# A contiguous 256 KiB head for each tensor in a streaming x + alpha * fx

## The chip, the cores and the metric

The kernel runs on one core of one Trainium2 chip. The metric is the device time of one execution in microseconds, as the median of several runs. A separate profiled execution gives the profile; its span runs from the core's first to its last instruction and is a little shorter than the time, which also holds what lies around it.

## The reference

```python
B, S, D = 512, 32, 640
# x, fx: bfloat16 of shape (B, S, D); alpha: bfloat16 of shape (1,)
def reference(x, fx, alpha):
    return x + alpha * fx
```

Each of x, fx and the output holds 10,485,760 elements, 20.97 MB. Two are read and one is written: 62.92 MB in all.

## The kernel before

**Layout.** Each tensor is seen as 128 rows of 81,920 contiguous elements, one row for each partition of the on-chip memory. A row is counted in units of K = 512 elements (1 KiB): it is ROW = 160 units long, 160 KiB, and that is also the distance in DRAM from one partition's row to the next. All numbers in the plan are such units.

**One buffer.** There is a single tile `t` (L77) of 160 + 47.5 = 207.5 units per partition. x 0 to 160 lies at places 0 to 160, the sum is written over x, and the output is stored from there. fx has no place of its own: each piece is loaded to a place that x does not need yet, or no longer needs, and `lies` remembers where it went. So fx 0 to 65 lies at 95 to 160, where x 95 to 160 is to come; fx 65 to 112.5 lies in the spare room from 160 to 207.5; and later pieces overwrite earlier ones there.

**An order written out by hand.** The string PLAN (L27 to L55) gives the program order, one step to a line, and each engine runs its own steps in this order:

- `f a b p` loads fx from a to b to place p (L99 to L101), `x a b` loads x (L96, L97), `s a b` stores (L119, L120). All of these, and the load of alpha, are issued by SP (SyncE) and go through one DMA queue. A load over a place that is still read, and a store of a sum that is not there yet, wait on SP, and everything behind them on SP waits too.
- `a` loads alpha (L103 to L111): its one element goes to 8 partitions, a 1 x 1 matrix multiplication with a row of ones on TensorE spreads it over 128 partitions, and VectorE copies it out of PSUM (L111).
- `m a b` multiplies fx by alpha in place on VectorE (L113, L114), and `c a b` adds it to x (L116, L117).
- `s 0 64 | m 112.5 134.5` also makes that store wait for the named multiplication (L129, L130).

The plan has three stretches. First the loads that need no room to be made: fx 0 to 8, alpha, fx 8 to 65, x 0 to 64, x 64 to 95 and fx 65 to 112.5. Then VectorE multiplies and adds piece by piece; x 95 to 112.5 and x 112.5 to 160 are issued when fx 0 to 65 has been added, and the last two pieces of fx when fx 65 to 95 and 95 to 112.5 have been. Last the stores: 0 to 64 is issued while the last loads still run, then 64 to 128, then 128 to 160. A nop on SP (L132) waits for all but the last store.

`of` (L87, L88) cuts units a to b out of a tensor in DRAM, `at` (L84, L85) cuts them out of `t`, and `place` (L90 to L94) finds where a piece of fx lies. A transfer over 128 partitions becomes 128 pieces, one for each partition, spread over 16 DMA engines, so each engine moves eight.

Of the kernel before, what the change touches and what calls it, by code (L numbers as in the profile page):

```python
# [1 line left out]

# [4 lines left out]

ALU = mybir.AluOpType
F32 = mybir.dt.float32

P = 128
K = 512
ROW = 160
SPARE = 47.5

LANES = 8

PLAN = """  # L27
f 0 8 95
a
f 8 65 103  # L30
x 0 64
x 64 95
f 65 112.5 160
m 0 8
m 8 65
c 0 8
c 8 64
c 64 65
x 95 112.5
x 112.5 160  # L40
m 65 95
c 65 95
f 112.5 142.5 160
m 95 112.5
c 95 112.5
f 142.5 160 190
m 112.5 134.5
s 0 64 | m 112.5 134.5
m 134.5 142.5
c 112.5 142.5  # L50
m 142.5 160
c 142.5 160
s 64 128
s 128 160
"""  # L55


@with_exitstack
def kernel(
    ctx: ExitStack,  # L60
    tc: tile.TileContext,
    x: bass.AP,
    fx: bass.AP,
    alpha: bass.AP,
    out: bass.AP,
):
    nc = tc.nc
    xv, fv, ov = (
        t.flatten_outer_dims().rearrange("(p n) d -> p (n d)", p=P) for t in (x, fx, out)
    )  # L70
    assert xv.shape[1] == ROW * K

    consts = ctx.enter_context(tc.tile_pool(name="consts", bufs=1))
    psum = ctx.enter_context(tc.tile_pool(name="psum", bufs=1, space=bass.MemoryType.PSUM))
    flat = ctx.enter_context(tc.tile_pool(name="flat", bufs=1))
    ctx.enter_context(tc.manual_schedule())
    t = flat.tile([P, int((ROW + SPARE) * K)], x.dtype, name="t")  # L77
    info = mybir.DependencyInfo(mybir.DependencyClass.Sync, mybir.DependencyReason.DATA)

    lanes = {}  # L80
    lies = []
    done = []

    def at(a, b):  # L84
        return t[:, int(a * K) : int(b * K)]  # L85

    def of(v, a, b):  # L87
        return v[:, int(a * K) : int(b * K)]  # L88

    def place(a, b):  # L90
        for c, d, p in reversed(lies):
            if c <= a and b <= d:
                return at(p + a - c, p + b - c)
        raise ValueError(f"fx {a} to {b} lies nowhere in one piece")  # L94

    def load_x(a, b):  # L96
        done.append(nc.sync.dma_start(out=at(a, b), in_=of(xv, a, b)))  # L97

    def load_f(a, b, p):  # L99
        lies.append((a, b, p))  # L100
        done.append(nc.sync.dma_start(out=at(p, p + b - a), in_=of(fv, a, b)))  # L101

    def load_alpha():  # L103
        a_n = consts.tile([LANES, 1], alpha.dtype, name="a_n")
        done.append(nc.sync.dma_start(out=a_n[:], in_=alpha[None, :].to_broadcast([LANES, 1])))  # L105
        ones = consts.tile([1, P], alpha.dtype, name="ones")
        nc.vector.memset(ones[:], 1.0)  # L107
        a_ps = psum.tile([P, 1], F32, name="a_ps")
        done.append(nc.tensor.matmul(a_ps[:], ones[:], a_n[0:1, :], start=True, stop=True))  # L109
        lanes["a"] = consts.tile([P, 1], F32, name="a_f")  # L110
        nc.vector.tensor_copy(out=lanes["a"][:], in_=a_ps[:])  # L111

    def multiply(a, b):  # L113
        done.append(nc.vector.tensor_scalar_mul(place(a, b), place(a, b), lanes["a"][:]))  # L114

    def add(a, b):  # L116
        done.append(nc.vector.tensor_add(at(a, b), at(a, b), place(a, b)))  # L117

    def store(a, b):  # L119
        done.append(nc.sync.dma_start(out=of(ov, a, b), in_=at(a, b)))  # L120

    does = {"x": load_x, "f": load_f, "a": load_alpha, "m": multiply, "c": add, "s": store}
    begun = {}
    for step in filter(None, PLAN.split("\n")):
        step, *later = step.split(" | ")
        what, *numbers = step.split()
        does[what](*map(float, numbers))
        begun[step] = done[-1]
        for other in later:  # L129
            tc.add_manual_dep(done[-1].ins, begun[other].ins.name, info, reason="begins late")  # L130

    rest = nc.sync.nop(nofuse=True)  # L132
    for i in done[:-1]:
        tc.add_manual_dep(rest.ins, i.ins.name, info, reason="all but the last store")


# [1 line left out]
_INS = ['x', 'fx', 'alpha']  # L138
_OUTS = [((512, 32, 640), 'bfloat16')]


# [23 lines left out]
```

## Time and profile before

| | |
|---|---|
| median of 3 runs (lowest to highest) | 151.05 us (151.03 to 151.10) |
| profiled execution | 151.06 us, of it a span of 149.3 us |
| VectorE busy | 66.5 us, 16 instructions |
| TensorE, ScalarE, GpSimd busy | 0.2 us or less each |
| DMA: HBM read and written | 41.94 MB and 20.97 MB, 421 GB/s over the span |
| fx 0 to 8, from issue to landing | 5.0 us, 1024 KB |
| fx 8 to 65, from issue to landing | 21.3 us, 7296 KB |

The DMA queue is one queue in order, so the time from issue to landing of a transfer holds the time of those ahead of it. The profile counts packets (one contiguous piece that one DMA engine moves) and says what share of time the 16 engines spent on them. Where a stretch of time is cut out, a packet is counted where it starts, so short stretches with long packets can show more or less than the true rate. Idle time of VectorE is put down to the load for which it waited.

### The profile page before, as it was taken

The page shows a single profiled execution, that of the slowest core. Times are in us where ns is not written, and L with a number is a line of the kernel's source. Part 1 is how long each engine was busy: PE and PEld are TensorE (multiplying, and loading weights), DVE is VectorE, ACT ScalarE, POOL GpSimd, SP SyncE. Part 2 cuts the span into 40 slices and gives each one's busy share as a digit, 9 for nine tenths or more (in the row PEclk, how much of TensorE's full clock was granted, in tenths as well). Part 3 has the DMA queues.
Part 4 walks back from the last instruction along what each step waited for, and adds up shares of the span by engine and source line. Part 5 has one row for each costly group of instructions (what it writes and reads, how often), then busy time and mean ns, then how long its engine had stood idle before and what let it go on. Part 6 is the DMA issues. An engine that isn't in the chain of part 4 may idle for free.

```text
span 149.3 us, 85 instructions
## 1 busy us (share of the span) xinstructions
PE 0.2 (0%) x1; PEld 0.1 (0%) x1; DVE 66.5 (45%) x16; POOL 0.2 (0%) x4
## 2 busy tenths in 40 slices
PE   0000000000000000000000000000000000000000
PEld 0000000000000000000000000000000000000000
DVE  0300008920069999029999900599997000000000
POOL 0000000000000000000000000000000000000000
DMA  5969998969699999999999799899896969697994
GB/s 149 617 266 500 500 461 351 562 281 562 281 408 442 447 417 443 456 388 565 430 417 417 340 461 461 379 516 457 386 562 281 562 281 562 281 562 334 430 439 202
DMA packets 1745, 62.92 MB, mean 421 GB/s; under 512 B 209, under 2 KB 209, under 8 KB 209
## 3 DMA queue, kind: packets, MB, share of 16 engines
q1 hardware_dynamic: 1744, 62.92, 98.1%
q14 instruction: 1, 0.00, 0.0%
HBM read 41.94 MB, written 20.97 MB: 421 GB/s over the span
## 4 chain that ended last, share of the span: by engine, by line
DMA 38%; DVE 31%; another core or an unknown queue 4%; issue 2%; SPq 1%; DVEq 0%
DMA t<-in_x_dram 27%; DVE t L117 26%; DMA t<-in_fx_dram 11%; DVE t L114 5%; SPq L101 0%; SPq L105 0%; DVEq L117 0%
## 5 line engine op out<-in xcount | busy, mean ns | idle before, releaser
L117 DVE TENSOR_TENSOR t<-t 128x15360 bf16<-128x15360 bf16 (+4 forms) x7 | 43.6, 6251 | 11.7 <-DMA t<-in_x_dram 11.6
L114 DVE TENSOR_SCALAR t<-t,a_f 128x4096 bf16<-128x4096 bf16 (+4 forms) x7 | 22.8, 3265 | 30.7 <-DMA t<-in_fx_dram 30.7
L111 DVE COPY a_f<-a_ps 128x1 f32<-128x1 f32 x1 | 0.2, 158 | 5.0 <-PE a_ps L109 5.0
L107 DVE MEMSET ones<- 1x128 bf16 x1 | 0.2, 165 | 0.8 <-PEq L149 0.8
L109 PE MATMUL a_ps<-a_n,ones 1*128 1x1 bf16 x1 | 0.2, 158 | 5.8 <-DMA a_n<-in_alpha_dram 5.8
L149 POOL MEMSET const-bfloat16-1.0<- 128x1 bf16 x1 | 0.1, 101 | 0.0
L149 POOL MEMSET const-uint8-127<- 128x1 uint8 x1 | 0.1, 101 | 0.0
L109 PEld LDWEIGHTS <-ones 1*128 1x128 bf16 x1 | 0.1, 99 | 1.0 <-DVE ones L107 1.0
L149 POOL MEMSET const-float32-0.0<- 128x1 f32 x1 | 0.1, 98 | 0.2 <-issue 0.2
L149 POOL MEMSET const-float32-1.0<- 128x1 f32 x1 | 0.1, 98 | 0.0
## 6 DMA issues: line engine op xcount, KB each, us to landing
t<-in_fx_dram SPq DMA_DIRECT2D x1, 7296.0 KB, 21.3
t<-in_fx_dram SPq DMA_DIRECT2D x1, 6080.0 KB, 63.0
t<-in_x_dram SPq DMA_DIRECT2D x1, 6080.0 KB, 25.7
out_dram<-t SPq DMA_DIRECT2D x1, 4096.0 KB, 33.7
t<-in_x_dram SPq DMA_DIRECT2D x1, 3968.0 KB, 49.2
t<-in_fx_dram SPq DMA_DIRECT2D x1, 3840.0 KB, 16.4
t<-in_x_dram SPq DMA_DIRECT2D x1, 2240.0 KB, 11.7
t<-in_fx_dram SPq DMA_DIRECT2D x1, 2240.0 KB
```

The source lines that it names most:

```text
L107: nc.vector.memset(ones[:], 1.0)
L109: done.append(nc.tensor.matmul(a_ps[:], ones[:], a_n[0:1, :], start=True, stop=True))
L111: nc.vector.tensor_copy(out=lanes["a"][:], in_=a_ps[:])
L114: done.append(nc.vector.tensor_scalar_mul(place(a, b), place(a, b), lanes["a"][:]))
L117: done.append(nc.vector.tensor_add(at(a, b), at(a, b), place(a, b)))
L149: nc = _bacc.Bacc("TRN2", target_bir_lowering=False, num_devices=1)
```

## The change

The units 0 to 2 of all 128 partitions, 2 KiB each, no longer come from the heads of 128 rows that lie 160 KiB apart. They come from the first 256 KiB of each tensor, which lie in one piece; the rest of the tensor is cut into 128 rows of 158 units, which lie 158 KiB apart. As the operation is elementwise and all three tensors are cut in the same way, the output is the same.

The first load is then fx 0 to 2 in place of 0 to 8. The second is fx 2 to 65 (it was third, as 8 to 65), and alpha comes third. x 2 to 66 is loaded ahead of x 0 to 2, and the store 2 to 66 goes ahead of the store 0 to 2, since a transfer cannot cross from the head to the rest. The multiplications are cut at 2 in place of 8; of the additions, 0 to 8, 8 to 64 and 64 to 65 become 2 to 65 and 0 to 2. Beside alpha's there were nine loads and three stores; there are now ten and four.

```diff
+HEAD = 2
...
 PLAN = """
-f 0 8 95
+f 0 2 95
+f 2 65 97
 a
-f 8 65 103
-x 0 64
-x 64 95
+x 2 66
+x 0 2
+x 66 95
 f 65 112.5 160
-m 0 8
-m 8 65
-c 0 8
-c 8 64
-c 64 65
+m 0 2
+m 2 65
+c 2 65
+c 0 2
 x 95 112.5
 x 112.5 160
 m 65 95
...
 c 95 112.5
 f 142.5 160 190
 m 112.5 134.5
-s 0 64 | m 112.5 134.5
+s 2 66 | m 112.5 134.5
 m 134.5 142.5
 c 112.5 142.5
 m 142.5 160
 c 142.5 160
-s 64 128
-s 128 160
+s 0 2
+s 66 130
+s 130 160
 """
...
-    xv, fv, ov = (
-        t.flatten_outer_dims().rearrange("(p n) d -> p (n d)", p=P) for t in (x, fx, out)
-    )
-    assert xv.shape[1] == ROW * K
+    xv, fv, ov = (t.flatten_outer_dims().rearrange("n d -> (n d)") for t in (x, fx, out))
+    assert xv.shape[0] == P * ROW * K
...
     def of(v, a, b):
-        return v[:, int(a * K) : int(b * K)]
+        assert b <= HEAD or a >= HEAD
+        at_head = b <= HEAD
+        part = v[: int(P * HEAD * K)] if at_head else v[int(P * HEAD * K) :]
+        shift = 0 if at_head else HEAD
+        return part.rearrange("(p n) -> p n", p=P)[:, int((a - shift) * K) : int((b - shift) * K)]
```

## The prediction

> **What bounds the kernel now.** I read the page first, the busy shares by slice, the one DMA queue and the chain, then the order of time, then stretches of half a microsecond at the start.
>
> ```profile
> span 149.3 us, 85 instructions
> ...
> DMA  5969998969699999999999799899896969697994
> ...
> q1 hardware_dynamic: 1744, 62.92, 98.1%
> ...
> DMA 38%; DVE 31%; another core or an unknown queue 4%; issue 2%; SPq 1%; DVEq 0%
> ```
>
> The reader is to see one queue that is full for 98.1% of the span. The chain gives 31% to VectorE, yet this does not make VectorE the bound: the chain steps through an addition because it releases a later load's issue, while the queue still has other loads to move. The lines by time show how far ahead the issues are.
>
> ```profile
> 0.73 0.38 SPq L101 DMA_DIRECT2D t<-in_fx_dram  x1
> ...
> 1.16 0.35 SPq L105 DMA_DIRECT2D a_n<-in_alpha_dram  x1
> 1.57 0.35 SPq L101 DMA_DIRECT2D t<-in_fx_dram  x1
> 1.96 1.04 SPq L97 DMA_DIRECT2D t<-in_x_dram  x2
> 3.05 0.53 SPq L101 DMA_DIRECT2D t<-in_fx_dram  x1
> ...
> 22.93 7.82 DVE L114 TENSOR_SCALAR t<-t,a_f 128x29184 bf16<-128x29184 bf16 x1 [15.49 <-DMA t<-in_fx_dram]
> 42.34 17.63 DVE L117 TENSOR_TENSOR t<-t 128x4096 bf16<-128x4096 bf16 x3 [11.60 <-DMA t<-in_x_dram]
> 59.66 0.80 SPq L97 DMA_DIRECT2D t<-in_x_dram  x2
> 66.07 4.22 DVE L114 TENSOR_SCALAR t<-t,a_f 128x15360 bf16<-128x15360 bf16 x1 [6.10 <-DMA t<-in_fx_dram]
> ```
>
> The loads issued at 59.66 stand behind fx 65 to 112.5, which lands at 66.07; so that issue has 6.4 us in hand, less the 1.0 us from an issue to its first packet (0.73 to 1.74 for the first load in the packet records). The only stretch in which the queue has work and does not run full is the first:
>
> ```profile
> 1.00:1.50 0.50, 0.00 (x0) 0.10 (x1) 0.00 (x0) 0.00 (x0) 1.00 0.00 0
> 1.50:2.00 0.50, 0.00 (x0) 0.00 (x0) 0.00 (x0) 0.00 (x0) 1.00 1.59 262
> 2.00:2.50 0.50, 0.00 (x0) 0.00 (x0) 0.00 (x0) 0.00 (x0) 1.00 0.42 82
> 2.50:3.00 0.50, 0.00 (x0) 0.00 (x0) 0.00 (x0) 0.00 (x0) 1.00 0.78 246
> 3.00:3.50 0.50, 0.00 (x0) 0.00 (x0) 0.00 (x0) 0.00 (x0) 1.00 0.85 328
> 3.50:4.00 0.50, 0.00 (x0) 0.00 (x0) 0.00 (x0) 0.00 (x0) 1.00 1.02 426
> ```
>
> The last column is GB/s: 197 on the mean from 1.5 to 3.0, 426 by 3.5. (A packet counts where it starts.) In the packet records each engine moves eight 8 KiB packets of the first load. The later ones all take about 309 ns, but the first of each engine takes 793 ns on the mean (342 to 1253), a loss of 0.48 us; all eight together lose 0.75 us on the mean, and 1.07 us on the engine that ends last (884 and 802 ns for its first two). From then on nothing is made up: engines leave the first load 0.54 us apart and end the kernel 0.6 us apart.
>
> This lets the span be rebuilt. The 64 KiB and 8 KiB packets (2418 and 309 ns) give 36.8 ns per KiB and engine, or 435 GB/s: 62.92 MB is 144.6 us. Twelve transfers of 8 packets per engine, each packet with about 5 ns more that do not depend on its size, and a semaphore write of some 10 ns per transfer, are 0.6. With 1.74 to the first packet, 1.07 of slow start, 0.36 from the last packet to its landing and 0.75 of ending this makes 149.1, against 149.3. Outside the span lie 151.06 - 149.3 = 1.76 us; the profiled execution's 151.06 stands 0.01 above the median of 151.05.
>
> **The change part by part.** *Bytes.* The same 62.92 MB move: 0.
>
> *Transfers.* Twelve large ones become fourteen (one more load of x, one more store), with three of 2 KiB packets: fx, x and out 0 to 2. Per engine that adds 16 packets and 2 semaphore writes. No 2 KiB packet is in the trace. From below, the 64 KiB rate makes it 75 ns; from above, a 4-byte packet takes 9 ns, so 75 + 9 = 84. I take 5 ns of fixed cost, as between 8 and 64 KiB: 16 x 5 + 2 x 6 = **+0.09 us** (0 to +0.17). It lies in a full queue, so it is on the path.
>
> *The start.* The first load is 256 KiB in one piece instead of 128 rows 160 KiB apart. This is the term that decides, and no row shows it. Upper end of the gain: the slowest engine's 1.07 goes, less up to 0.17 because engines start up to 0.23 us apart: 0.9. Lower end: no gain; below nothing, if the next load's first rows pay a first packet's 0.48 on top. I take neither. Two engines had first packets of 342 and 399 ns, nearly the settled time, and lost 686 and 383 ns in their second: the loss is not one fixed delay of waking up, it goes with opening rows that lie apart. The small load opens far fewer; its successor opens one row per engine. So I leave one first packet's mean loss, 0.48, and the gain is 1.07 - 0.48 = **-0.59 us**.
>
> The Trainium skill (DMA: Bandwidth & Descriptors, Latency and other measured facts) reports that 128 rows at pitches of large powers of two fall to 207 GB/s and less, and that a few KiB of padding restore the rate. Here 160 KiB runs at 435 after the start, so the trace does not bear it out beyond 3.5 us; if it were the cause of the 197, the new pitch of 158 KiB would clear all of the loss and the time would be 150.25 instead.
>
> *The second load must be there.* It moves from third issue to second: 1.16 instead of 1.57 us, first packets from 1.16 + 1.0 = 2.2. The head needs 8 x 84 ns = 0.67 us from 1.74 to 1.97, so until 2.4 to 2.6 without any slow packet. There is no gap: 0. Left behind alpha it would come at 2.6.
>
> *Alpha third.* Its packets now queue behind 8 of 63 KiB (2.32 us each), so it lands at about 22 us instead of 5.7. Behind it stand the matrix multiplication, the copy (L109, L111) and all VectorE work. The multiplications then begin at 22.9 + 0.4 for matmul and copy (5.72 to 6.15 now), with 1024 elements in 0.48 us (4096 in 1.28, 29184 in 7.82, so 0.26 ns each) and 32256 in 8.62: done by 32.5. What they feed waits until x lands at 42.3. Cover of some 10 us: 0. Without it, 0.4 + 0.48 + 8.62 - 7.82 = 1.7 us.
>
> *The additions.*
>
> ```profile
> L117 DVE TENSOR_TENSOR t<-t 128x28672 bf16<-128x28672 bf16 x1 | 15.1, 15083 | 0.0
> ...
> L117 DVE TENSOR_TENSOR t<-t 128x4096 bf16<-128x4096 bf16 x1 | 2.3, 2293 | 11.6 <-DMA t<-in_x_dram 11.6
> L117 DVE TENSOR_TENSOR t<-t 128x512 bf16<-128x512 bf16 x1 | 0.4, 416 | 0.0
> ```
>
> At 0.52 ns per element, 2 to 65 takes 16.95 and 0 to 2 takes 0.68, together 17.63, what the three took. Both loads of x that wait for their space (95 to 112.5 on both additions) issue near 60.0 instead of 59.66 and 60.04: 0.3 of 5 us in hand: 0. Behind them on SP stands only the issue at 78.5, which waits for later work anyway.
>
> *Issues.* SP issues seven loads in a row instead of six, about 0.5 us more, by some 4.1 us; the third large one is needed at 22: 0. The store 0 to 2 waits for nothing new behind store 2 to 66 at 98.1, and 66 to 130 issues at 107.5 while the queue still stores 2 to 66 until 119: 0. Later work keeps its forms and its distance to the landings.
>
> Sum: 149.3 + 0.09 - 0.59 = 148.8; with 1.76 outside, 150.56, less 0.01 for the median: **150.55 us**.
>
> **The rivals.** *The slow start is a matter of time, not of rows* (engines or memory ramp up for about 1.5 us whatever is read). For it: every engine is settled by 3.8 us, however its loss was spread. Against it: the 342 ns packet. Then only the 0.09 remains: 151.14.
>
> *The start is paid twice, the case on the other side.* The head goes through its slow packets and then the second load opens 128 fresh rows with little queued ahead. If each engine loses a mean first packet's 0.48 again, the time is 151.05 + 0.09 + 0.48 = 151.6. It decides as soon as that second loss exceeds what the head saves, less 0.09. Against it: x 0 to 64, also 128 fresh rows, shows packets of 2418 to 2472 ns, no loss; but it stood behind 17 us of packets.
>
> *Every added transfer exposes its latency.* Two more, each with 1.0 us from issue to first packet and 0.36 to landing, would be +2.7: 153.8. Against it: fx 8 to 65 landed at 22.9, 17.2 us after its forerunner, 435 GB/s with nothing between. The Trainium skill's DMA page (Anatomy of one DMA) has about 2 us fixed per DMA, so by that rule 4 us more; it speaks against small transfers, and the queue of this trace does not agree.
>
> *The change does not do what it says*: a piece of 256 KiB is cut in four packets of 64 KiB on four engines. These would move 2.42 us instead of 0.67 for each of three transfers: +5.3, 156.4. The packet count would tell.
>
> **How the numbers follow.** Forecast 0.65, of which 0.05 falls above 150.75; time not rows 0.18; paid twice 0.11; latencies 0.02; cut otherwise 0.04. About 0.2% is what a measurement can tell here, 0.3 us. Faster: 0.60. Within: 0.05 + 0.18 = 0.23. Slower: 0.11 + 0.02 + 0.04 = 0.17. The likeliest case's own range is 150.1 (0.9 gained, nothing paid) to 150.9; with the rivals up to 151.6, the range is 150.1 to 151.6.
>
> **What would show it.** In the new profile: 1792 large packets; the first packet near 1.74; a rate near 400 GB/s before 3.0 us; fx 2 to 65 landing near 22.3; 2 KiB packets of x and out at 80 to 84 ns; alpha's copy near 22.5; all later landings earlier by the same half microsecond. I am wrong if the first rates stay below 250 GB/s until 3.0, if the second load's first packets take well over 2.4 us, or if the gain of the start is lost at a later landing.

## The result and the profile after

The changed kernel takes 151.35 us (median of 21 runs, 151.18 to 151.72) against 151.07 for the kernel before (21 runs, 150.98 to 151.24): a ratio of 1.0018, with a 95% interval of 1.0012 to 1.0024. It is 0.28 us slower, where 0.50 faster was forecast. Its profiled execution took 151.44 us.

The changed kernel's page, its span and its DMA part:

```profile
span 149.7 us, 87 instructions
...
DMA  9697998969699999989999899999696979696993
...
DMA packets 2032, 62.92 MB, mean 420 GB/s; under 512 B 240, under 2 KB 240, under 8 KB 624
...
q1 hardware_dynamic: 2032, 62.92, 98.0%
```

The queue is as full as before. 2032 packets less the 240 tiny ones are 1792, of which 384 (624 - 240) are the 2 KiB packets of three transfers: the change was built as it reads, fourteen transfers of 128 packets. The order of time of the changed kernel shows where the difference arises (start, duration, what, and the idle time before it):

```profile
0.72 0.85 SPq L107 DMA_DIRECT2D t<-in_fx_dram  x2
...
1.63 0.36 SPq L111 DMA_DIRECT2D a_n<-in_alpha_dram  x1
...
22.98 0.16 PE L115 MATMUL a_ps<-a_n,ones 1*128 1x1 bf16 x1 [22.98 <-DMA a_n<-in_alpha_dram]
...
23.37 9.02 DVE L120 TENSOR_SCALAR t<-t,a_f 128x1024 bf16<-128x1024 bf16 x2
42.68 17.56 DVE L123 TENSOR_TENSOR t<-t 128x32256 bf16<-128x32256 bf16 x2 [10.30 <-DMA t<-in_x_dram]
60.27 0.80 SPq L103 DMA_DIRECT2D t<-in_x_dram  x2
66.44 4.22 DVE L120 TENSOR_SCALAR t<-t,a_f 128x15360 bf16<-128x15360 bf16 x1 [6.20 <-DMA t<-in_fx_dram]
...
95.28 4.35 DVE L120 TENSOR_SCALAR t<-t,a_f 128x11264 bf16<-128x11264 bf16 x2 [9.10 <-DMA t<-in_fx_dram]
```

The three lines that wait for a load begin at 42.68, 66.44 and 95.28; before, they began at 42.34, 66.07 and 94.91. The third of these lines in the kernel before:

```profile
94.91 4.35 DVE L114 TENSOR_SCALAR t<-t,a_f 128x11264 bf16<-128x11264 bf16 x2 [9.10 <-DMA t<-in_fx_dram]
```

The delay is 0.34, 0.37 and 0.37 us: it is there at the first landing of x, and nothing that comes later adds more than 0.03. So the answer lies in the first stretches, here of the changed kernel (last column GB/s):

```profile
1.50:2.00 0.50, 0.00 (x0) 0.00 (x0) 0.00 (x0) 0.00 (x0) 1.00 0.67 98
2.00:2.50 0.50, 0.00 (x0) 0.00 (x0) 0.00 (x0) 0.00 (x0) 1.00 0.72 209
2.50:3.00 0.50, 0.00 (x0) 0.00 (x0) 0.00 (x0) 0.00 (x0) 1.00 6.19 2282
3.00:3.50 0.50, 0.00 (x0) 0.00 (x0) 0.00 (x0) 0.00 (x0) 1.00 0.00 0
```

The first two stretches together are no faster than before (98 and 209 GB/s against 262 and 82). The 2282 is no rate: all 16 engines begin a 63 KiB packet there, and a packet counts where it starts. The packet records tell the rest. The head's packets should take 84 ns; eight of those begun between 1.83 and 1.89 us take 446 to 468 ns and all end between 2.28 and 2.35 us. Over its eight packets an engine loses 0.31 us on the mean. The first 63 KiB packets, settled at 2380 ns, then take 2566 to 3349, another 0.45 on the mean over the second load. Sum 0.76, against 0.75 before. In these two profiles the mean loss is the same, only divided between two loads; what has changed is that one engine loses 0.97 us in a single packet.

To compare starts I use one figure from the packet records: when each engine's last packet of fx 0 to 65 ended, less 19.67 us, the settled time of that engine's share (19.71 where the load is cut in three). Call it the effective start, and the difference between first and last engine the spread.

| profile | first packets | mean | slowest | spread |
|---|---|---|---|---|
| before | 8 KiB | 2.60 | 2.87 | 0.53 us |
| changed | 2 KiB, then 63 KiB | 2.62 | 3.19 | 0.88 us |

The slowest engine is 0.32 us later. With the 0.09 for two added transfers that makes 0.41, against 0.37 between the two spans (149.281 and 149.655).

### The profile page after: what moved, and what is told of

Same layout as the page of the kernel before. It is cut to its first block, busy times and chain, and to the rows that moved or that the text cites. A ratio compares the mean times of both kernels' runs of the same rounds, so it can differ in the third digit from the quotient of the medians.

```text
span 149.7 us, 87 instructions
## 1 busy us (share of the span) xinstructions
PE 0.2 (0%) x1; PEld 0.1 (0%) x1; DVE 66.4 (44%) x15; POOL 0.2 (0%) x4
## 2 busy tenths in 40 slices
DMA packets 2032, 62.92 MB, mean 420 GB/s; under 512 B 240, under 2 KB 240, under 8 KB 624
## 3 DMA queue, kind: packets, MB, share of 16 engines
q1 hardware_dynamic: 2032, 62.92, 98.0%
## 4 chain that ended last, share of the span: by engine, by line
DMA 38%; DVE 31%; another core or an unknown queue 4%; issue 2%; SPq 1%; DVEq 0%
DMA t<-in_x_dram 27%; DVE t L123 26%; DMA t<-in_fx_dram 11%; DVE t L120 5%; SPq L107 1%; SPq L111 0%; DVEq L123 0%
## 5 line engine op out<-in xcount | busy, mean ns | idle before, releaser
L123 DVE TENSOR_TENSOR t<-t 128x15360 bf16<-128x15360 bf16 (+3 forms) x6 | 43.5, 7268 | 10.4 <-DMA t<-in_x_dram 10.3
L120 DVE TENSOR_SCALAR t<-t,a_f 128x8960 bf16<-128x8960 bf16 (+5 forms) x7 | 22.7, 3264 | 15.3 <-DMA t<-in_fx_dram 15.3
```

## The experiments

Three theories were set against each other. *Rows*: the loss is paid where an engine opens a row far from those that it has read (the ground on which the prediction stood). *Time*: it belongs to the first microseconds, whatever is read. *Step*: 16 engines that begin long packets together collide. A fourth, *spread*, came out of these runs. Ratios are to the kernel before in runs on the same chip, with 95% intervals.

**Is it the contiguous piece?**

```diff
# head_in_rows: the changed plan, head and rest from the same rows, 160 KiB apart
     def of(v, a, b):
+        return v.rearrange("(p n) -> p n", p=P)[:, int(a * K) : int(b * K)]
```

> The changed plan, but with units 0 to 2 taken from the rows at 160 KiB pitch as before, not from a contiguous piece. In the changed kernel the first load lost 0.31 us per engine on the mean against settled packets and the second 0.45. Theory rows (the loss is paid where an engine opens a row that lies far from those it has read): the head now opens all 128 rows, so the first load loses more, 0.5 us or over, and the second load, which goes on in the same rows, loses under 0.1; sum about 0.75. Theory time (some 1.5 us of slow start whatever is read): the second load loses about 0.45 again. Theory step (16 engines start long packets within 0.25 us of each other and collide): the second load also loses about 0.45. Time within 0.1 us of the changed kernel, 151.35, by all three.

1.0016 (1.0000 to 1.0032), 151.35 us. The head lost 0.24 us per engine and the second load 0.34, although it went on in rows that the head had just opened. The rows theory wanted under 0.1 there: it falls at this point, and neither the contiguous piece of 256 KiB nor the pitch of 158 KiB makes a difference that these runs can tell.

**Does a later second load escape?**

```diff
# head_four_times
+w 0 2 2
+w 0 2 4
+w 0 2 6
 f 0 2 95
 f 2 65 97
```

(`w` loads fx 0 to 2 to the place named last.)

> The changed kernel with the contiguous 256 KiB head of fx loaded three times more, to places that x fills later, ahead of everything. It adds 0.75 MiB of traffic, about 2 us, so the second large load starts near 4.8 us in place of 2.7. Theory rows: its first packets, which open 128 fresh rows, again lose about 0.45 us on the mean. Theory step: the same. Theory time: by 4.8 us the start is over, and they lose under 0.1.

A single run, 153.4 us. The four small loads lost 0.20, 0.05, 0.10 and 0.03 us, and the second large one, from 4.75 us on, 0.20: neither 0.45 nor under 0.1. With a gap of 0.15 us ahead of the third small load besides, this run decides nothing. It fits no theory well: its 63 KiB packets begin from 4.75 to 5.45 us, when the start should be over, and its engines leave fx 2 to 65 0.92 us apart, of which 0.70 was there when the first of these packets began.

**Fresh rows with the queue full.**

```diff
# x_head_first
-x 2 66
-x 0 2
+x 0 2
+x 2 66
```

> The changed kernel with x 0 to 2 loaded ahead of x 2 to 66. Near 22.5 us, with the queue full, eight short packets per engine from a contiguous 256 KiB are then followed by 64 KiB packets that open 128 rows of x for the first time, as fx's were at 2.7 us. Theory rows: the first 64 KiB packets of x lose 0.15 to 0.45 us on the mean, and the time grows by as much. Theory step: engines are 0.5 us and more apart here, so under 0.05. Theory time: under 0.05, no change of time.

All 128 packets of x 2 to 66, the first of them begun at 22.5 us, take 2418 ns: a loss of 0.00. Short contiguous packets followed by long ones on 128 fresh rows cost nothing once the start is over. Rows falls for good. The ratio of 1.0027 (1.0014 to 1.0041) is not told from the changed kernel's on that chip, below.

**A larger head, so that the second load comes after the start.**

```diff
# head_of_8 (loads, stores and plan steps cut at 8 and 72)
-HEAD = 2
+HEAD = 8
-f 0 2 95
-f 2 65 97
+f 0 8 95
+f 8 65 103
```

> The changed kernel with a contiguous head of 8 units, 1 MiB per tensor, in place of 2: packets of 8 KiB, and the second load, which opens 128 fresh rows, begins near 4.8 us. Theory rows: the first load loses little and the second 0.2 to 0.45. Theory time: the first load loses 0.45 to 0.75, as 8 KiB packets from rows did, and the second under 0.05, as it begins after the start is over. Time by both 0.05 to 0.2 above the kernel before, by the two added transfers.

> The changed kernel itself, for a second profile and more times beside the other runs of this chip. First load and second load together lost 0.76 us per engine on the mean in its first profile, the head in rows 0.58, the kernel before with alpha third 0.46. If the sum belongs to the kernel, it is near 0.76 again; if it belongs to the execution, it lies anywhere from 0.45 to 0.8. Time 0.1 to 0.25% above the kernel before.

1.0019 (1.0010 to 1.0027). The first load, one contiguous MiB, lost 0.84 us and the second 0.01. That is what time says, if a little above its 0.45 to 0.75, and a contiguous piece did not help at all. The changed kernel beside it: 1.0019 (1.0011 to 1.0028), its loads losing 0.15 and 0.32. Together that is 0.47 and not 0.76, so by the expectation the sum belongs to the execution and not to the kernel. Its first packet came only at 1.94 us there; the mean effective start of 2.56 is still close to the 2.62 of its first profile, as the smaller loss makes up for the late first packet.

**Long packets from the first.**

```diff
# no_first_piece
-f 0 8 95
+f 0 65 95
 a
-f 8 65 103
```

> The kernel before with fx 0 to 65 as one first load instead of 0 to 8 and 8 to 65; its packets hold 32 KiB or more. Theory time: the same mean loss of 0.45 to 0.75 us, now within the first packets, and a time within 0.1 of the kernel before. Theory step (long packets that begin together collide): more than 0.75, and slower by 0.1 or more.

1.0051 (1.0039 to 1.0063), 0.7 us slower with one transfer less. The mean loss is 0.79 us, which time has and step, with its more than 0.75, cannot be told from; and yet the time is not the same: engines leave fx 65 with a spread of 1.14 us, the slowest with an effective start of 3.42. From here on the theory is *spread*: the mean loss is about given, the slowest engine sets the end, and a long packet that begins inside the slow start leaves one engine far behind.

**The parts of the change alone.**

```diff
# two_more_transfers: the kernel before, x and store cut at 2
-x 0 64
+x 2 64
+x 0 2
...
# alpha_third_alone: the kernel before
-a
 f 8 65 103
+a
...
# start_alone: the kernel before, in rows, 12 transfers
-f 0 8 95
-a
-f 8 65 103
+f 0 2 95
+f 2 65 97
+a
```

> The kernel before, with x 0 64 cut into 2 64 and 0 2, and the store 0 64 cut the same way, all in rows: the two added transfers alone. By the prediction's term of 5 ns for each packet and 6 for each semaphore write this costs 0.09 us: 151.16. If the added transfers are the whole difference of the changed kernel, 0.28: 151.35. The start is untouched: mean loss of the first load 0.75 us as before.

> The kernel before with x and the store cut into 2 to 64 and 0 to 2, once more. Its ratio was 1.0011 (0.9999 to 1.0023). By the prediction's term 1.0006; if transfers carry most of the change, 1.0012 or more.

> The kernel before with fx 8 to 65 issued second and alpha third, nothing else. Expected no change, 151.07 within 0.1: VectorE's multiplications begin near 23.3 us and end near 32.5, long before x lands at 42.3. If a late alpha is a part of the difference, the time is near 151.35.

> The kernel before with alpha third alone, once more, beside first pieces of 2, 4 and 16 on one chip. Its ratio was 0.9990 (0.9982 to 0.9999). Expected again 0.9985 to 1.0000, and a spread of engines of 0.4 to 0.6 us.

> The kernel before with a first load of fx 0 to 2 from the rows, fx 2 to 65 second and alpha third; x and the stores uncut, so 12 transfers as before and no contiguous piece. So far the slow start costs an engine about the same on the mean in every kernel, but engines leave it 0.30 to 0.56 us apart after 8 KiB packets, 0.70 to 0.88 after 2 KiB packets followed by 63 KiB ones, and 1.14 after 32.5 KiB ones. Theory spread (the slowest engine's longer start is most of what the change costs): 0.1 to 0.2 us slower than the kernel before, engines 0.7 us or more apart after fx 2 to 65. Theory transfers (the two added transfers are all of it): same time as before within 0.05.

> The start of 2 KiB packets alone, once more. Theory spread: 1.0010 to 1.0024, engines 0.7 to 1.1 us apart after fx 2 to 65, mean effective start not earlier than in the cushioned form by more than 0.1 us.

| kernel | ratio (95% interval) | mean, slowest, spread of the start |
|---|---|---|
| two_more_transfers | 1.0011 (0.9999 to 1.0023) | 2.45, 2.67, 0.39 us |
| two_more_again | 1.0006 (0.9994 to 1.0019) | 2.39, 2.90, 0.73 us |
| alpha_third_alone | 0.9990 (0.9982 to 0.9999) | 2.33, 2.65, 0.56 us |
| alpha_third_again | 0.9994 (0.9985 to 1.0002) | 2.41, 2.61, 0.41 us |
| start_alone | 1.0016 (1.0007 to 1.0024) | 2.57, 3.27, 1.09 us |
| start_alone_again | 1.0015 (1.0006 to 1.0024) | 2.65, 3.17, 0.88 us |

The start alone, with no contiguous piece and no added transfer, costs 0.15 to 0.16%, nearly the whole of the change's 0.18. Alpha third costs nothing, and may gain some 0.1%; as the start alone also has alpha third, the start itself costs rather more, 0.32 us on the chip that ran both (151.16 against 150.84). The added transfers cost between nothing and 0.2%, with the predicted 0.06% well inside. The first load of two_more_transfers, the same as that of the kernel before, lost 0.43 us and not the 0.75 that was expected. Five profiles with 8 KiB packets from rows lost 0.43 to 0.52 there: the one profile on which the prediction was built had an unusually large loss.

**Does the size of the first packets matter, or what follows them?**

```diff
# first_piece_4, and first_piece_16 in the same way, on start_alone
-f 0 2 95
-f 2 65 97
+f 0 4 95
+f 4 65 99
...
# start_cushioned, on start_alone
 f 0 2 95
-f 2 65 97
+f 2 10 97
+f 10 65 105
```

> The same with a first load of 0 to 4 and 4 KiB packets. Theory spread: the second load begins near 3.5 us, when most of the slow start is over; engines 0.4 to 0.7 us apart, time between that of a first piece of 2 and of 8, 0 to 0.1 us above before. Theory transfers: same as before within 0.05.

> The same with a first load of 0 to 16 and 16 KiB packets, so that longer packets meet the slow start. Theory spread: engines 0.5 to 0.8 us apart after fx 16 to 65, 0.05 to 0.2 us slower than alpha third with a first piece of 8. Theory transfers: same within 0.05.

> The start of 2 KiB packets (1.0016, engines 1.09 us apart after fx 65) with fx 2 to 65 cut into 2 to 10 and 10 to 65, so that packets of 8 KiB, not of 63 KiB, begin between 2.6 and 3.4 us. One more transfer, 13, priced at 0.05 us. Theory spread: the engines are 0.3 to 0.55 us apart again, and the time falls to that of the kernel before within 0.1. If short first packets by themselves cost the time, it stays 0.2 us or more above.

> The cushioned form on the same chip. Theory spread: at least 0.15 us below the uncushioned form although it has one more transfer, within 0.1 us of the kernel before, engines 0.3 to 0.6 us apart. If the two take the same time, what costs the time is the short first load itself.

| kernel | ratio (95% interval) | mean, slowest, spread of the start |
|---|---|---|
| first_piece_4 | 0.9999 (0.9989 to 1.0008) | 2.38, 2.57, 0.40 us |
| first_piece_16 | 0.9999 (0.9991 to 1.0008) | 2.48, 2.78, 0.53 us |
| start_cushioned | 1.0002 (0.9988 to 1.0017) | 2.33, 2.59, 0.49 us |
| start_cushioned_again | 0.9997 (0.9988 to 1.0006) | 2.49, 2.86, 0.56 us |

The cushioned start begins with the same 2 KiB packets and has one more transfer; only that 8 KiB packets, not 63 KiB ones, are begun from 2.6 to 3.1 us. On one chip it took 151.03 us and the uncushioned one 151.29. In order of time, the uncushioned start (again) and then the cushioned one (again), where VectorE waits for fx 65 to 112.5:

```profile
66.37 4.22 DVE L114 TENSOR_SCALAR t<-t,a_f 128x15360 bf16<-128x15360 bf16 x1 [6.10 <-DMA t<-in_fx_dram]
```

```profile
66.08 4.22 DVE L117 TENSOR_SCALAR t<-t,a_f 128x15360 bf16<-128x15360 bf16 x1 [6.02 <-DMA t<-in_fx_dram]
```

The reader is to see 0.29 us in hand at 66 us with one transfer more: the long packets in the slow start are what costs. With 16 KiB first packets the median is 150.98, which is 0.14 above alpha third with 8 KiB ones on the same chip (150.84) and inside the expected 0.05 to 0.2. The intervals overlap, so this small cost is not shown; against the kernel before there is none.

These runs also speak against step. In first_piece_4 the engines begin their first 61 KiB packet between 3.37 and 3.83 us, no further apart than their first 63 KiB packet in start_alone_again (2.64 to 3.15 us). There it loses 0.38 us on the mean, here 0.02. The loss goes with when long packets begin, not with their beginning together.

**What does the contiguous MiB cost?**

```diff
# cut_at_8_in_rows, on head_of_8
     def of(v, a, b):
+        return v.rearrange("(p n) -> p n", p=P)[:, int(a * K) : int(b * K)]
```

> The kernel with a head of 8 (14 transfers, all cut at 8), but with the pieces 0 to 8 taken from rows 160 KiB apart and not from a contiguous MiB. Alpha third with a first piece of 8 took 0.9990 and 0.9994. With 0.09 us for two transfers: 0.9998 to 1.0002. If the contiguous piece is what makes a head of 8 slow, this is near that and head_of_8_again stays at 1.0019; if the added transfers are, both are near 1.0019.

> The same kernel as head_of_8, beside its form in rows on one chip. Its ratio was 1.0019 (1.0010 to 1.0027), its mean loss in the first load 0.84 us per engine. If the contiguous piece makes the start worse, the loss is above that of the form in rows by 0.2 us or more; if that was the one execution, the two are alike.

In rows 0.9996 (0.9984 to 1.0008), 150.97 us, effective start 2.38 on the mean; contiguous 1.0016 (1.0003 to 1.0029), 151.30 us, 2.57 here and 2.68 in its first profile. Fourteen transfers cost nothing that can be told from the kernel before. The stretches at the start, first of the form in rows, then of the contiguous one in its first profile:

```profile
1.50:2.00 0.50, 0.00 (x0) 0.00 (x0) 0.00 (x0) 0.00 (x0) 1.00 1.30 262
2.00:2.50 0.50, 0.00 (x0) 0.00 (x0) 0.00 (x0) 0.00 (x0) 1.00 0.55 147
2.50:3.00 0.50, 0.00 (x0) 0.00 (x0) 0.00 (x0) 0.00 (x0) 1.00 0.85 328
```

```profile
1.50:2.00 0.50, 0.00 (x0) 0.00 (x0) 0.00 (x0) 0.00 (x0) 1.00 2.03 262
2.00:2.50 0.50, 0.00 (x0) 0.00 (x0) 0.00 (x0) 0.00 (x0) 1.00 0.27 33
2.50:3.00 0.50, 0.00 (x0) 0.00 (x0) 0.00 (x0) 0.00 (x0) 1.00 0.27 98
```

Both start 16 packets at once. Then the contiguous form starts two and six in the next two stretches (33 and 98 GB/s of 8 KiB packets), the form in rows nine and twenty. So in this profile a contiguous MiB starts worse than rows 160 KiB apart. In its second profile the loss was 0.34 + 0.05, not 0.2 above that of the form in rows (0.51 + 0.04), as it should have been if the contiguous piece made the start worse; its first packets came as late as 2.47 us instead. The slowest engine's effective start is 2.80 and 2.91 us, against 2.74 in rows. That the contiguous form takes longer is in the times (0.33 us on one chip, though the two intervals touch); that the start of fx is the cause is not shown, as this form also cuts x and the output in this way and leaves their other rows 152 KiB apart.

**Which engine counts, over all profiles.** Leave out the single run with three added loads, and 19 profiles remain. In 18 of them the span less the slowest engine's effective start is 146.38 to 146.53 us; in head_of_8's first it is 146.66. The span less the mean effective start lies anywhere from 146.58 to 147.15. So the engine that leaves the start last sets the span, and nearly all else is alike. The little that is left goes with the number of transfers: 146.41 on the mean of seven profiles with twelve, 146.50 on the mean of nine with fourteen. By this the two added transfers cost some 0.08 us, where 0.09 was predicted.

## Why the prediction was wrong, point by point

**The step that failed** is the start: "it goes with opening rows that lie apart", -0.59 us. Two short first packets, each followed by a slow second one, were read as a mark of rows (the records have a third, of 399 ns, followed by a loss of 332). head_in_rows, x_head_first and head_of_8 show that the mean loss does not follow rows: it is 0.3 to 0.85 us in every kernel, and with the queue full at 22.5 us even fresh rows cost 0.00. Between the two profiles the term measured 0.02 us on the mean and +0.32 on the slowest engine. The 1.07 of the slowest engine, from one execution, was taken as what could be won; that the sizes of the first packets and of those behind them also set how unevenly the loss falls was not thought of. The wider comparison agrees in size: over the six profiles with 63 KiB packets in the start the slowest engine's effective start is 3.08 us on the mean, over ten others in rows (4, 8 or 16 KiB, or cushioned) 2.72, so 0.35 later. But the mean moves with it, from 2.42 to 2.57: some 0.14 of the 0.35 is a larger mean, and the rest is spread. With +0.32 in place of -0.59, the sum is 149.3 + 0.09 + 0.32 + 1.76 = 151.5, against the 151.44 of the profiled execution and a median of 151.35.

**The rivals.** "A matter of time, not of rows" had the mechanism, as far as these runs show one, and gave 151.14; it lacked the spread. "Paid twice" named the right place, the second load's first packets, 2.57 to 3.35 us instead of 2.38, but the mean is divided, not doubled, and it lies 0.25 too high. The added transfers do not expose a latency: two of them cost 0.09 and 0.17 us by the medians of their ratios, not 2.7. The Trainium skill's 2 us per DMA (DMA: Bandwidth & Descriptors, Anatomy of one DMA), which the page gives for transfers that GpSimd issues, is likewise not seen here, where SP issues them and the queue runs on from one transfer to the next. The Trainium skill's pitch rule (DMA: Bandwidth & Descriptors, Latency and other measured facts) was stretched in the prediction: it is for pitches of 512 KiB and larger powers of two, and its 207 GB/s is for copies from DRAM to DRAM that reach 214 at full rate. As the prediction applied it, the pitch of 158 KiB would have cleared the slow start; the mean effective start of 2.62 against 2.60 does not agree.

**What held.** The rows of the changed kernel by form:

```profile
L123 DVE TENSOR_TENSOR t<-t 128x32256 bf16<-128x32256 bf16 x1 | 17.0, 16959 | 10.3 <-DMA t<-in_x_dram 10.3
...
L120 DVE TENSOR_SCALAR t<-t,a_f 128x32256 bf16<-128x32256 bf16 x1 | 8.6, 8616 | 0.0
...
L123 DVE TENSOR_TENSOR t<-t 128x1024 bf16<-128x1024 bf16 x1 | 0.7, 684 | 0.0
L120 DVE TENSOR_SCALAR t<-t,a_f 128x1024 bf16<-128x1024 bf16 x1 | 0.5, 486 | 0.0
```

16.95, 8.62, 0.68 and 0.48 were worked out. The multiplications end at 32.4, where 32.5 was forecast, with 10 us of cover. Alpha lands at 22.98, later than "about 22". One reason is a unit: the prediction's 36.8 ns are for 1000 bytes, and a KiB takes 37.7 (2418 less 309 ns over 56 KiB), so that a 63 KiB packet takes 2.38 us and not 2.32; its 435 GB/s and its sum for the span are right. The two loads that wait for space issue at 60.27, 0.3 later than forecast, ahead of 66.4. The second load's packets follow the head's without a gap. The 2 KiB packets of x and out take 84 ns, the upper end of 75 to 84, and the transfers' term of 0.09 is close to the 0.08 of the profiles.

**What stays open.** Why the first microseconds are slow at all; why long packets share that loss so unevenly; why the long packets of head_four_times still lost 0.20 us from 4.75 us on; and why a head of a contiguous MiB takes longer than one in rows.

## What to carry to other kernels

In this kernel, whose one queue is full from end to end, the end is set by the DMA engine that left the start last (to within 0.15 us in 18 of 19 profiles): in a kernel like it, look at the spread of the engines, not only at the mean rate. A loss at the start is not won by moving fewer bytes in it if it belongs to time; keep the packets that begin in it short, and the long ones out until it is over. Before a term is built on a loss, test what it follows: one run that swapped two loads in the middle of the kernel (x_head_first) would have shown that rows were not it.

## What the runs showed of the hardware that was not expected

The slow start costs an engine 0.3 to 0.85 us on the mean (19 profiles) whether it begins with packets of 2, 4, 8, 16 or 32.5 KiB, from rows or from one piece. The span follows the engine that leaves it last: the difference of the two is 146.38 to 146.53 us in 18 of 19 profiles. Beginning 63 KiB packets inside it, from 2.5 to 3.5 us, leaves the engines 0.70 to 1.09 us apart after 22 us (six profiles), 32.5 KiB ones 1.14 (one), while 4 to 16 KiB packets or a cushion of 8 KiB ones leave them 0.39 to 0.73 (in rows, ten). The uneven start alone costs 0.15 and 0.16%. Alpha's load between the first two loads costs no more than some 0.1%, and the plain kernel with alpha third (150.84 us twice, beside 150.98 and 150.93) is the fastest that ran, by a margin that the intervals hardly tell from none.
